# A fused attention and two-layer MLP kernel: the first stage in a new order, the layer-norm weights moved into the weight split, and new first loads

## The chip, the cores and the metric

The kernel runs on one core of a Trainium2 chip. The metric is the device time of one execution in microseconds (us); the kernel before takes 528.44 us (median of 3 runs, 527.57 to 528.45).

The engines are named as the profile names them: PE (TensorE: matmuls; PEld is its weight load), DVE (VectorE), ACT (ScalarE), POOL (GpSimd) and SP (SyncE, which here only starts DMAs). ACT can start DMAs too.

## The reference

Three steps, each feeding the next; the reference computes them in 32-bit floats (weights arrive as 64-bit floats).

```python
# 1. attention: batch 2, 8 heads, 768 positions, head size 64, n_global=8, n_local=96
scores = scale * q @ k^T
keep = (column < n_global) | (0 <= row - column < n_local)
scores = scores - slope[head] * dist          # dist: n_local for global columns, else |row - column|
a = softmax(where(keep, scores, -1e9)); x = a @ v          # x: 1536 tokens x 512
# 2. first layer: d_ff = 1024
h = x @ w_in; u = h * softmax(h)
ln = (u - mean(u)) / sqrt(var(u) + 1e-6) * g_ln
x2 = ln @ w_out
# 3. second layer: d_ff = 2048
g = x2w * sigmoid(x2w) with x2w = x2 @ w2_in;  out = g @ w2_out
```

## The kernel before

The 1536 tokens are 12 tiles of 128; tiles 0 and 6 begin a batch and see one key tile, the others two (their own and the one before). Each 32-bit matmul of the two layers is done as three matmuls of halves: both operands are split in a high part `hi` and a remainder `lo`, and hi*hi + hi*lo + lo*hi is summed in PSUM.

**The weights** come as 64-bit words in units of 128x512 numbers (512 KB). Units 0 to 7 are `w_in` (0 to 3 for the first 512 columns, 4 to 7 for the rest), 8 to 15 `w_out`, 16 and up the second layer. Each unit is loaded (`u_load`, five buffers), its upper words scaled (`u_exp`, on POOL, ACT or DVE), put together by three bit passes on DVE (`u_bits`, L139, L141, L143), and split (`u_hi`, L124 or L126; `u_lo`, L162). The units of `w_out` are multiplied by `g_ln` between (`u_gain`, L154).

**The first stage**, for each tile: scores of heads 0 to 3 and of heads 4 to 7 (`scores`, L275); on DVE the bias and the row's maximum for each head (`smax`, L294); on ACT exp with the row's sum (`sexp`, L300); two small DVE instructions for the sums' reciprocals (`ssum`); the multiplication of each head by it (`snorm`, on POOL or DVE, L126: called a norm below); transposes (L322), their copies out of PSUM (`transA_out`, ACT), the product with v (`av`, L341), its split (ACT, then DVE); then the two halves of the hidden layer (`hmm`, L380, 12 matmuls each), the layer norm (`ln_max`, `ln_exp`, `ln_u`, `ln_s`, `ln_sq`, `ln_c` with a power of -0.5 on POOL, L420; `ln_d` on POOL, L424 and L425), its transpose (L435), and, for two tiles together, the two halves of `w_out` (`x2`, L455, 48 matmuls each).

**The order of the work** is written out: `ORDER` is a list of some 860 tokens such as `d3:5` (bias and maximum of head 3, tile 5), which Python calls one after another. Each engine executes its own instructions in that order; a wait on one engine holds all that stands behind it there. The same holds for the two DMA queues (SP and ACT). PSUM has four buffers `p`, so a group of matmuls also waits until an earlier group has been read. Ahead of the list stand the loads of the two counts (`ints`, L629 and L630) and the masks.

**The second stage** (from the matmuls of L518 on) runs in two groups of 768 tokens; the remaining units are prepared in its background.

Of the kernel before, what the change touches and what calls it, by code (L numbers as in the profile page):

```python
# [53 lines left out]


@with_exitstack
def kernel(ctx, tc, q, k, v, n_global, n_local, w_in, w_out, g_ln, w2_in, w2_out, out):
    nc = tc.nc
    B, H, S, D = 2, 8, 768, 64
    NT, DM = out.shape  # L60
    FF = w_in.shape[1]
    FF2 = w2_in.shape[1]
    NTILE = NT // 128
    TB = S // 128
    KD = DM // 128
    KF = FF // 128
# [791 lines left out]
```

## Time and profile before

| | |
|---|---|
| median of 3 runs | 528.44 us (527.57 to 528.45) |
| the profiled execution | 527.69 us; its span 525.6 us |
| PE busy | 495.4 us, 94% of the span |
| DVE, ACT, POOL busy | 311.9, 236.4 and 157.7 us |
| PE's share of the chain that ended last | 88% |

The page shows the span in 40 slices of 13.1 us: PE stands at 9 tenths or more from the fourth slice to the last but one, with one slice at 7 (near 225 us). A busy PE is not PE at its peak: the granted clock has a row of its own and is below full speed in the third slice.

### The profile page before, as it was taken

How to read it: one execution, taken by the hardware profiler on the slowest of the kernel's cores; microseconds unless marked ns; L12 is line 12 of the kernel's file. 1: busy time of each engine (PE TensorE's matmuls, PEld its weight loads, DVE VectorE, ACT ScalarE, POOL GpSimd, SP SyncE). 2: the span in 40 equal slices, each digit the busy share in tenths (PEclk: the TensorE clock that was granted, in tenths of full speed). 3: DMA queues.
4: the chain of work that ended last, by engine and by line, in shares of the span. 5: the costliest groups of instructions: out<-in, count | busy, mean ns of one | idle time of the engine just before them, and what ended most of it. 6: DMA issues, size and time to landing. Idle time of an engine off the chain costs nothing.

```text
span 525.6 us, 8114 instructions
## 1 busy us (share of the span) xinstructions
PE 495.4 (94%) x3025; PEld 436.1 (83%) x3025; DVE 311.9 (59%) x721; ACT 236.4 (45%) x532; POOL 157.7 (30%) x205
## 2 busy tenths in 40 slices
PE   1779999999999999979999999999999999999993
PEld 1457778889889889879999898989899898989982
DVE  4868888966566767974569898883441313122231
ACT  4866778554555645623245545443431212222121
POOL 2787968932222334151223242332000000000000
PEclk9969999999999999999999999999999999999998
DMA  7955524321304100202133433300030000000003
GB/s 197 296 168 144 172 67 122 101 63 59 121 1 141 42 19 24 81 4 77 42 98 110 153 108 133 121 1 2 0 121 2 0 1 0 1 0 1 1 1 126
DMA packets 27488, 38.37 MB, mean 73 GB/s; under 512 B 2864, under 2 KB 15152, under 8 KB 27440
## 3 DMA queue, kind: packets, MB, share of 16 engines
q1 hardware_dynamic: 27296, 37.24, 22.7%
q8 instruction: 26, 0.43, 0.3%
q10 hardware_dynamic: 144, 0.52, 0.3%
q14 instruction: 22, 0.18, 0.1%
HBM read 34.61 MB, written 3.15 MB: 72 GB/s over the span
## 4 chain that ended last, share of the span: by engine, by line
PE 88%; DVE 4%; POOL 3%; issue 2%; SPq 1%; DMA 1%; ACT 0%; DVEq 0%; POOLq 0%
PE p L518 26%; PE p L569 25%; PE p L455 12%; PE p L380 10%; PE p L275 4%; PE p L322 4%; PE p L341 4%; PE p L435 2%; DMA rq<-in_q_dram 1%; POOL st L420 1%; DVE A L294 1%; POOL A L126 1%; SPq L119 1%; POOL e L425 1%; DVE st L390 0%
## 5 line engine op out<-in xcount | busy, mean ns | idle before, releaser
L533 DVE SCALAR_TENSOR_TENSOR e<-e,p 128x384 f32<-128x384 f32 x64 | 32.6, 551 | 125.8 <-ACT e L527 125.8
L527 ACT ACTIVATE e<-p 128x384 f32<-128x384 f32 x64 | 28.0, 489 | 134.0 <-PE p L518 134.0
L569 PE MATMUL p<-w3h,gl 128*128 128x512 f32 x192 | 75.8, 395 | 0.0
L569 PE MATMUL p<-w3l,gh 128*128 128x512 f32 x192 | 75.7, 394 | 0.0
L569 PE MATMUL p<-w3h,gh 128*128 128x512 f32 x192 | 75.4, 393 | 0.0
L143 DVE SCALAR_TENSOR_TENSOR cc<-cx,cc 128x512 uint32<-128x512 uint32 x48 | 58.5, 1221 | 0.2
L518 PE MATMUL p<-x2h,w2h 128*128 128x384 f32 x256 | 55.6, 338 | 0.0
L518 PE MATMUL p<-x2l,w2h 128*128 128x384 f32 x256 | 55.5, 338 | 0.0
L518 PE MATMUL p<-x2h,w2l 128*128 128x384 f32 x256 | 55.4, 338 | 0.0
L300 ACT ACTIVATE A<-A,negmax 128x256 f32<-128x256 f32 (+1 forms) x96 | 46.2, 483 | 14.3 <-DVE negmax L294 13.9
L380 PE MATMUL p<-wih,xT 128*128 128x512 f32 x192 | 50.7, 406 | 0.0
L126 POOL TENSOR_SCALAR A<-A,sm 128x256 f32<-128x256 f32 (+1 forms) x71 | 40.5, 582 | 31.1 <-DVE sm L305 25.9
L518 PEld LDWEIGHTS p<-x2h,w2h 128*128 128x128 f32 x256 | 46.1, 188 | 2.6
L518 PEld LDWEIGHTS p<-x2l,w2h 128*128 128x128 f32 x256 | 46.0, 188 | 0.0
L518 PEld LDWEIGHTS p<-x2h,w2l 128*128 128x128 f32 x256 | 45.8, 188 | 0.0
L294 DVE CUSTOM_DVE_ANT_0 A<-p,bias 128x256 f32<-128x256 f32 (+1 forms) x96 | 34.8, 395 | 16.9 <-PE p L322 6.3
L569 PEld LDWEIGHTS p<-w3h,gl 128*128 128x128 f32 x192 | 36.1, 188 | 8.3
L569 PEld LDWEIGHTS p<-w3l,gh 128*128 128x128 f32 x192 | 36.0, 188 | 7.3
L569 PEld LDWEIGHTS p<-w3h,gh 128*128 128x128 f32 x192 | 36.1, 188 | 7.2
L380 PEld LDWEIGHTS p<-wih,xT 128*128 128x128 f32 x192 | 34.5, 189 | 9.0 <-issue 1.7
L275 PE MATMUL p<-rk,rq 64*128 64x256 f32 (+1 forms) x192 | 29.6, 441 | 11.2 <-DMA rk<-in_k_dram 9.0
L162 POOL TENSOR_TENSOR w3l<-cc,w3h 128x512 fp32r<-128x512 f32 x16 | 23.5, 1468 | 52.0 <-ACT w3h L124 48.6
(106 smaller groups left out, 839.6 us busy)
## 6 DMA issues: line engine op xcount, KB each, us to landing
cx<-in_moe_w_out_dram SPq DMA_DIRECT2D x24, 512.0 KB, 3.4
cx<-in_moe_w_in_dram SPq DMA_DIRECT2D x23, 512.0 KB, 3.8
rq<-in_q_dram SPq DMA_DIRECT2D x12, 256.0 KB, 4.6
rk<-in_k_dram SPq DMA_DIRECT2D x12, 256.0 KB, 4.9
vf<-in_v_dram SPq DMA_DIRECT2D x12, 256.0 KB, 5.4
out_dram<-x2T SPq DMA_DIRECT2D x12, 256.0 KB, 3.2
cx<-in_moe_w_in_dram ACTq DMA_DIRECT2D x1, 512.0 KB, 5.6
ints<-in_n_local_dram SPq DMA_DIRECT2D x1, 1.0 KB, 5.0
```

The costliest lines, as they stand in the source:

```text
L126: eng.tensor_scalar(out=out, in0=in_, scalar1=scale, scalar2=1.0, op0=ALU.mult, op1=ALU.mult)
L143: V.scalar_tensor_tensor(out=y, in0=x[:, :, 1].bitcast(U32), scalar=0x80000000, in1=y, op0=ALU.bitwise_and, op1=ALU.bitwise_or)
L162: eng.tensor_tensor(out=lo, in0=w, in1=f(hi), op=ALU.subtract)
L275: nc.tensor.matmul(p[:, a, j, 0:128 * len(ks)], lhsT=rq[z, t % 2, pr, :], rhs=rk[z, W, pr, :], start=True, stop=True)
L294: nc.vector.tensor_tensor_reduce(out=x[:, c, 0:n], in0=p[:, a, j, 0:n], in1=bb, scale=-0.125, scalar=1e30, op0=ALU.add, op1=ALU.min, accum ...
L300: nc.scalar.activation(out=x[:, c, 0:n], in_=x[:, c, 0:n], func=ACTF.Exp, bias=negmax[:, t * H + h:t * H + h + 1], scale=-1.0, accum_out=s ...
L380: nc.tensor.matmul(p[:, half, :], lhsT=x[:, a, kk, :], rhs=w[:, kk, n], start=(i == 0), stop=(i == 11))
L455: nc.tensor.matmul(p[:, d], lhsT=x[:, kk, c], rhs=y[:, kk, sl], start=(i == 0), stop=(i == 3 * KF - 1))
L518: nc.tensor.matmul(p, lhsT=w[m // 2][:, kk, c], rhs=x[:, kk, s * HG:(s + 1) * HG], start=(i == 0), stop=(i == 11))
L527: nc.scalar.activation(out=e, in_=p2[:, s, 0:HG], func=ACTF.Tanh, scale=0.5)
L533: nc.vector.scalar_tensor_tensor(out=e, in0=e, scalar=1.0, in1=p2[:, s, 0:HG], op0=ALU.add, op1=ALU.mult)
L569: nc.tensor.matmul(o, lhsT=x[:, c], rhs=w[m // 2][:, m % 2, :], start=(m == 0 and i == 0), stop=(last and i == 2))
```

## The change

- `ORDER` is a new list; each token's work may move on its engine.
- **Norms on three engines**: `m0a` to `m7a` put a norm on ACT. Before, 71 of the 96 were on POOL and 25 on DVE; now 36 are on POOL, 34 on ACT and 26 on DVE.
- **Layer-norm weights**: `u_gain` is gone. `u_hi` of a `w_out` unit now multiplies by `g_ln` (two ACT instructions of 256 numbers in place of one of 512), and `u_lo` does so too (two DVE `scalar_tensor_tensor`). Before, seven of these eight units were multiplied and seven subtracted on POOL; now no `w_out` unit uses POOL for either.
- **First loads**: k of tiles 0 and 1 and unit 2 are started by ACT, the rest by SP; the two counts come as one row each and are spread over the 128 partitions by a matmul (`counts_all`, and a copy out of PSUM); `g_ln` comes as 8 rows of 128 numbers and is transposed by a matmul, where it was a load of 1,024 single numbers.
- **Masks**: the second set of bias products is spread over ACT, DVE and POOL (`bba`, `bbv`, `bbp`).
- **Layer norm**: the power and the following product are a token of their own (`lp`), and `ln_d` runs on POOL (7 tiles), ACT (3) or DVE (2).

The diff, cut to its core (the list of tokens to its first lines):

```diff
-cl:0 lq:0 lk:0 cep:0 c1:0 ba:0 sb:0 bb:0 c2:0 cl:1 sa:0 c3:0 d0:0 d4:0 cep:1 d1:0 d5:0 d2:0 lk:1 d6:0 c1:1 d3:0 lq:1 kg:0 c2:1 bc:0 cl:2 d7:0 lq:2
...
+ints:0 lka:0 ni:0 nb:0 lq:0 mk:0 cla:2 ml:0 cl:3 sb:0 bbv:6 bbp:7 sa:0 bbp:1 bbv:2 ba:0 lq:1 bbp:0 d0:0 lka:1 cep:2 d4:0 cl:0 x0:0 cl:6 d1:0 d5:0 d2:0
...
-    ints = per.tile([128, 4], I32, name="ints")
+    ints = per.tile([1, 4], I32, name="ints")
+    intf = per.tile([1, 4], F32, name="intf")
+    one = per.tile([1, 128], F32, name="one")
+    g8 = per.tile([8, 128], F32, name="g8")
...
-    def u_gain(i, eng):
-        w, g = u_parts(i)[0], units[i][3]
-        for j in range(units[i][1]):
-            eng.tensor_scalar(out=w[:, j], in0=w[:, j], scalar1=g[:, j:j + 1], scalar2=1.0, op0=ALU.mult, op1=ALU.mult)
-
     def u_hi(i, eng=None):
         w, hi, _ = u_parts(i)
-        scaled(hi, w, eng)
+        g = units[i][3]
+        if g is None:
+            scaled(hi, w, eng)
+        else:
+            for j in range(units[i][1]):
+                scaled(hi[:, j], w[:, j], eng, g[:, j:j + 1])
 
     def u_lo(i, eng):
         w, hi, lo = u_parts(i)
-        eng.tensor_tensor(out=lo, in0=w, in1=f(hi), op=ALU.subtract)
+        g = units[i][3]
+        if g is None:
+            eng.tensor_tensor(out=lo, in0=w, in1=f(hi), op=ALU.subtract)
+        else:
+            for j in range(units[i][1]):
+                eng.scalar_tensor_tensor(out=lo[:, j], in0=w[:, j], scalar=g[:, j:j + 1], in1=f(hi[:, j]), op0=ALU.mult, op1=ALU.subtract)
         ustate.pop(i)
...
+    def counts():
+        nc.sync.dma_start(out=ints[:, 0:2], in_=n_local.bitcast(I32).rearrange("(a n) -> a n", a=1))
+        nc.sync.dma_start(out=ints[:, 2:4], in_=n_global.bitcast(I32).rearrange("(a n) -> a n", a=1))
...
+    def counts_all():
+        mt["p"] = psum()[:, 0, 0:4]
+        nc.tensor.matmul(mt["p"], lhsT=one, rhs=intf, start=True, stop=True)
...
+    def gains():
+        nc.sync.dma_start(out=g8, in_=g_ln.rearrange("(k p) -> k p", p=128))
+
+    def gains_t():
+        mt["g"] = psum()[:, 0, 0:KF]
+        nc.tensor.transpose(mt["g"], g8, ident[0:KF, 0:KF])
...
-        nc.gpsimd.tensor_tensor(out=col[6], in0=col[6], in1=mhalf, op=ALU.pow)
-
-    def ln_d(t):
+
+    def ln_r(t):
         u, col = ys[t]
-        nc.gpsimd.tensor_tensor(out=col[6], in0=col[6], in1=col[4], op=ALU.mult)
-        nc.gpsimd.tensor_scalar(out=u, in0=u, scalar1=col[2], scalar2=col[6], op0=ALU.add, op1=ALU.mult)
+        P = nc.gpsimd
+        P.tensor_tensor(out=col[6], in0=col[6], in1=mhalf, op=ALU.pow)
+        P.tensor_tensor(out=col[6], in0=col[6], in1=col[4], op=ALU.mult)
+        if f"lda:{t}" in toks:
+            P.tensor_tensor(out=col[7], in0=col[6], in1=col[2], op=ALU.mult)
+
+    def ln_d(t, eng=None):
+        u, col = ys[t]
+        if eng is None:
+            nc.scalar.activation(out=u, in_=u, func=ACTF.Identity, bias=col[7], scale=col[6])
+        else:
+            eng.tensor_scalar(out=u, in0=u, scalar1=col[2], scalar2=col[6], op0=ALU.add, op1=ALU.mult)
         ys[t] = u
...
-        nc.sync.dma_start(out=ints[:, 0:2], in_=n_local.bitcast(I32).partition_broadcast(128))
-        nc.sync.dma_start(out=ints[:, 2:4], in_=n_global.bitcast(I32).partition_broadcast(128))
...
-            if x == "lk:0":
-                nc.sync.dma_start(out=gt, in_=g_ln.rearrange("(k p) -> p k", p=128))
```

How the order moves, in three places (each row is an instruction's line, its operation, what it writes and reads, its size, and how many follow each other).

ACT from its first instruction, before: `cx` is a weight unit, `bias_92` and `bias` the bias products, `A` the scores, `wih` a split unit, `ath` transposed scores copied out.

```order
L119 DMA cx<-in_moe_w_in_dram 128x1024
L124 ACT_TABLE_LOAD
L124 ACTIVATE bias_92<-dm 128x128 x8
L124 ACTIVATE bias<-dm 128x256 x8
L300 ACTIVATE A,sm<-A,negmax 128x128 x8
L124 ACTIVATE wih<-cc 128x512 x2
L124 ACTIVATE ath<-p 128x512
```

And now:

```order
L208 DMA rk<-in_k_dram 128x4x128
L123 DMA cx<-in_moe_w_in_dram 128x1024
L128 ACT_TABLE_LOAD
L128 ACTIVATE bias_95<-dm 128x128 x8
L208 DMA rk<-in_k_dram 128x4x128
L333 ACTIVATE A,sm<-A,negmax 128x128 x3
L128 ACTIVATE bias<-dm 128x256
L333 ACTIVATE A,sm<-A,negmax 128x128 x5
L128 ACTIVATE A<-A,sm 128x128 x3
L128 ACTIVATE wih<-cc 128x512
L128 ACTIVATE A<-A,sm 128x128 x2
```

The exps of tile 0 (L300, now L333) stand behind 8 and 1 bias products where they stood behind 16; k of tile 1 is started between them, and five norms of tile 0 (`A<-A,sm`) follow on ACT.

POOL, the norms of tiles 0 and 1, before: `wil` is the remainder of a `w_in` unit, `kg`, `rk` and `vg` copies of the global keys and values.

```order
L126 TENSOR_SCALAR A<-A,sm 128x128 x4
L126 TENSOR_SCALAR cc<-cx 128x512
L162 TENSOR_TENSOR wil<-cc,wih 128x512 x2
L126 TENSOR_SCALAR A<-A,sm 128x256 x7
L126 TENSOR_SCALAR vg<-vf 8x512
L126 TENSOR_SCALAR A<-A,sm 128x256
```

And now:

```order
L130 TENSOR_SCALAR A<-A,sm 128x128 x3
L168 TENSOR_TENSOR wil<-cc,wih 128x512
L130 TENSOR_SCALAR cc<-cx 128x512
L130 TENSOR_SCALAR rk<-kg 128x4x8
L168 TENSOR_TENSOR wil<-cc,wih 128x512
L130 TENSOR_SCALAR cc<-cx 128x512
L130 TENSOR_SCALAR A<-A,sm 128x256 x4
```

Tile 1 had all its eight norms (128x256) on POOL; now it has four there, three on ACT and one on DVE.

POOL near the end of the first stage, the layer norms of tiles 10 and 11, before: `st` holds the tile's small columns (L420 is the power), `e` the tile, `w3l` and `w2l` remainders of second-layer units.

```order
L420 TENSOR_TENSOR st<-st,mhalf 128x1
L162 TENSOR_TENSOR w3l_2271<-cc,w3h_2270 128x512
L424 TENSOR_TENSOR st<-st 128x1
L425 TENSOR_SCALAR e<-e,st 128x1024
L162 TENSOR_TENSOR w2l_2269<-cc,w2h_2268 128x512
L420 TENSOR_TENSOR st<-st,mhalf 128x1
L424 TENSOR_TENSOR st<-st 128x1
L425 TENSOR_SCALAR e<-e,st 128x1024
```

And now:

```order
L457 TENSOR_TENSOR st<-st,mhalf 128x1
L458 TENSOR_TENSOR st<-st 128x1
L460 TENSOR_TENSOR st<-st 128x1
L168 TENSOR_TENSOR w2l_2264<-cc,w2h_2263 128x512
L457 TENSOR_TENSOR st<-st,mhalf 128x1
L458 TENSOR_TENSOR st<-st 128x1
L467 TENSOR_SCALAR e<-e,st 128x1024
```

A remainder no longer stands between the power and the product; the large multiplication of tile 10 is gone from POOL (it is on ACT), that of tile 11 stays. On DVE the four subtractions of the second layer's input (L501, now L543), which stood together between the columns of tiles 10 and 11, stand two and two around tile 11's column.

## Rows read from the trace of the kernel before

**Rows 1.** By stretch: window, length, busy PE, PEld, DVE, ACT, POOL (xinstructions), clock, DMA.

```profile
0.00:9.00 9.00, 0.00 (x0) 0.02 (x1) 2.29 (x10) 1.30 (x2) 1.91 (x10) 1.00 0.59 149
9.00:40.90 31.90, 23.07 (x136) 17.02 (x137) 25.96 (x87) 24.17 (x78) 23.35 (x33) 0.84 0.76 240
40.90:109.50 68.60, 67.82 (x504) 55.67 (x503) 57.02 (x165) 50.90 (x121) 53.32 (x78) 1.00 0.38 111
109.50:220.00 110.50, 110.50 (x838) 95.41 (x837) 74.99 (x226) 58.03 (x134) 31.22 (x51) 1.00 0.20 61
220.00:236.00 16.00, 12.53 (x105) 12.32 (x104) 12.12 (x22) 6.78 (x11) 8.74 (x5) 1.00 0.09 33
236.00:517.00 281.00, 281.00 (x1449) 255.67 (x1449) 138.42 (x218) 94.64 (x188) 39.16 (x29) 1.00 0.14 47
```

**Rows 2.** What PE waited for in the whole span: total us, times, longest.

```profile
PE p L275 <- DMA rk<-in_k_dram: 9.0, 1, 9.0
PE p L322 <- POOL A L126: 4.6, 4, 3.4
PE p L435 <- POOL e L425: 3.6, 2, 3.5
PE p L341 <- DVE negmax L294: 2.5, 1, 2.5
PE p L275 <- DMA rq<-in_q_dram: 2.2, 1, 2.2
```

**Rows 3.** Timeline of POOL after 23 us: start, duration (us), instructions [idle before].

```profile
23.56 5.26 POOL L126 TENSOR_SCALAR A<-A,sm 128x256 f32<-128x256 f32 x7 [1.12 <-DVE sm L305]
```

**Rows 4.** Timeline near 225 us, POOL, DVE and PE.

```profile
221.71 4.48 POOL L420 TENSOR_TENSOR st<-st,mhalf 128x1 f32<-128x1 f32 x1 [10.87 <-DVE st L419]
...
222.22 3.55 DVE L501 TENSOR_TENSOR x2l<-x2T,x2h 128x768 fp32r<-128x768 f32 x4
...
229.38 1.10 PE L435 MATMUL p<-ident,e 128*128 128x128 f32 x8 [3.47 <-POOL e L425]
...
236.98 0.55 POOL L420 TENSOR_TENSOR st<-st,mhalf 128x1 f32<-128x1 f32 x1 [6.42 <-DVE st L419]
```

**Rows 5.** Timeline of SP, the queue of the first loads.

```profile
1.19 0.41 SPq L630 DMA_DIRECT2D ints<-in_n_global_dram  x1
...
3.22 3.75 SPq L119 DMA_DIRECT2D cx<-in_moe_w_in_dram  x1
```

**Rows 6.** DMA issues of the page: kind, count, KB each, median us to landing.

```profile
out_dram<-x2T SPq DMA_DIRECT2D x12, 256.0 KB, 3.2
```

**Rows 7.** Timeline of DVE in the first 12 us.

```profile
7.02 0.17 DVE L226 CAST nlf<-ints 128x4 f32<-128x4 int32 x1 [4.75 <-DMA ints<-in_n_global_dram]
...
9.26 0.42 DVE L139 TENSOR_SCALAR cc<-cc 128x512 uint32<-128x512 uint32 x1
...
10.44 0.69 DVE L143 SCALAR_TENSOR_TENSOR cc<-cx,cc 128x512 uint32<-128x512 uint32 x1
11.24 0.29 DVE L294 CUSTOM_DVE_ANT_0 A<-p,bias 128x128 f32<-128x128 f32 x1
```

**Rows 8.** Instructions to 109.5 us by line and form: count, busy us, mean ns, idle before.

```profile
L126 POOL TENSOR_SCALAR A<-A,sm 128x256 f32<-128x256 f32 x39 | 24.9, 651 | 6.9 <-DVE sm L305 4.0 <-ACT A L300 3.0
L143 DVE SCALAR_TENSOR_TENSOR cc<-cx,cc 128x512 uint32<-128x512 uint32 x16 | 13.4, 845 | 0.1
L141 DVE SCALAR_TENSOR_TENSOR cc<-cx,cc 128x512 uint32<-128x512 uint32 x16 | 12.9, 814 | 0.2
L162 POOL TENSOR_TENSOR wol<-cc,woh 128x512 fp32r<-128x512 f32 x7 | 10.5, 1507 | 0.0
L139 DVE TENSOR_SCALAR cc<-cc 128x512 uint32<-128x512 uint32 x16 | 9.2, 577 | 1.6 <-POOL cc L126 1.1 <-ACT cc L124 0.3
L154 POOL TENSOR_SCALAR cc<-cc,gt 128x256 f32<-128x256 f32 x14 | 7.9, 580 | 0.9 <-DVE cc L143 0.8
```

**Rows 9.** Timeline of ACT from 8 us.

```profile
8.98 4.16 ACT L124 ACTIVATE bias<-dm 128x128 bf16<-128x128 f32 x16 [6.53 <-DVE dm L234]
```

More of the change, by code (lines that the diff above doesn't have):

```diff
@@ L60 @@
     NT, DM = out.shape
+    toks = ORDER.split()
     FF = w_in.shape[1]
@@ L190, with load @@
     rq = at.tile([128, 2, H // 2, 128], F32, name="rq")
-    def load(nm, t):
+    def load(nm, t, eng=nc.sync):
         if nm == "v":
             vt[t] = at2.tile([128, DM], F32, tag="v", name="vf", bufs=4)
-            nc.sync.dma_start(out=vt[t], in_=v[t])
+            eng.dma_start(out=vt[t], in_=v[t])
         else:
@@ L243, in masks2 @@
-    def masks2(eng=None):
-        dm = dms[0]
-        for h in range(H):
-            scaled(bias[:, h, 0:2, :], dm[:, 0:2, :], eng, -(2.0 ** (2 - h)))
-    def masks3():
-        nc.vector.tensor_copy(bias[:, :, 2, :], bias[:, :, 0, :])
+        z = 2 if c else 0
+        if c:
+            V.tensor_copy(nlf, mt.pop("p"))
+        V.tensor_scalar(out=mk[:, c, :], in0=rf[:, c, :], scalar1=nl, scalar2=1e30, op0=ALU.is_ge, op1=ALU.mult)
+        V.scalar_tensor_tensor(out=mk[:, z, :], in0=rf[:, 2, :], scalar=ng, in1=mk[:, c, :], op0=ALU.is_ge, op1=ALU.mult)
@@ new lines, in mask_rows, with bias_first, bias_head @@
+        if c:
+            V.scalar_tensor_tensor(out=dm[:, 2, :], in0=rf[:, 1, :], scalar=nl, in1=mk[:, 2, :], op0=ALU.min, op1=ALU.max)
+        else:
+            V.scalar_tensor_tensor(out=dm[:, 0:2, :], in0=rf[:, 0:2, :], scalar=nl, in1=mk[:, 0:2, :], op0=ALU.min, op1=ALU.max)
+    def bias_first():
+        for h in range(H):
+            scaled(bias0[:, h, :], mt["dm"][:, 2, :], None, -(2.0 ** (2 - h)))
+    def bias_head(h, eng=None):
+        scaled(bias[:, h, 0:2, :], mt["dm"][:, 0:2, :], eng, -(2.0 ** (2 - h)))
@@ L600 @@
     OPS = dict(
-        lk=lambda t: load("k", t), lq=lambda t: load("q", t), lv=lambda t: load("v", t),
-        ba=lambda t: masks1(), bb=lambda t: masks2(), bc=lambda t: masks3(),
+        ints=lambda _: counts(), ni=lambda _: counts_f(), nb=lambda _: counts_all(), mk=lambda _: mask_rows(1), ml=lambda _: mask_rows(0),
+        ba=lambda _: bias_first(), g8=lambda _: gains(), gm=lambda _: gains_t(), gt=lambda _: gains_out(), cl=u_load, cla=lambda i: u_load(i, nc.scalar),
         kg=k_global, vg=v_global, sa=lambda t: scores(t, 0), sb=lambda t: scores(t, 1),
@@ L617 @@
     )
+    for n in "qkv":
+        OPS[f"l{n}"] = lambda t, n=n: load(n, t)
+        OPS[f"l{n}a"] = lambda t, n=n: load(n, t, nc.scalar)
+    for e, eng in (("a", None), ("v", V_), ("p", P_)):
+        OPS[f"bb{e}"] = lambda h, eng=eng: bias_head(h, eng)
+        OPS[f"bc{e}"] = lambda _, eng=eng: bias_wrap(eng)
+        OPS[f"ld{e}"] = lambda t, eng=eng: ln_d(t, eng)
     for i in range(8):
+        OPS[f"m{i}a"] = lambda t, i=i: snorm(t, i, None)
         OPS[f"d{i}"] = lambda t, i=i: smax(t, i)
@@ L628 @@
     with tc.manual_schedule():
-        nc.sync.dma_start(out=ints[:, 0:2], in_=n_local.bitcast(I32).partition_broadcast(128))
-        nc.sync.dma_start(out=ints[:, 2:4], in_=n_global.bitcast(I32).partition_broadcast(128))
         masks()
-        for x in ORDER.split():
+        for x in toks:
             nm, t = x.split(":")
```

122 lines of the change are left out of this document (61 added, 61 removed).

## The prediction

> **What bounds the kernel now.** I read the busy time by stretch first [rows 1]. From 236 us on PE is busy all the time (281.00 of 281.00), and the change moves nothing there but the background units; from 109.5 to 220 us it is busy 110.50 of 110.50. So all that can be won stands in three places: the 9.0 us before the first matmul, the 31.9 us after it with PE busy 23.07 and a granted clock that averages 0.84, and the 16 us from 220 us with PE busy 12.53. After 40.9 us PE hardly waits, so what the first stage wins by then it keeps only if no later matmul has to wait; a later wait is lost for good.
>
> Then the list of PE's waits [rows 2]: 9.0 us for the first keys, 2.2 us for the second queries, 4.6 us for norms on POOL, 2.5 us at the product with v, and 3.6 us for the layer norm on POOL. Two rows show the causes. In the timeline of POOL seven norms of tile 1 follow one another for 5.26 us while PE waits [rows 3]. Near 225 us a power of 128x1 numbers takes 4.48 us where the next one takes 0.55; beside it DVE runs four subtractions for 3.55 us, and PE then waits 3.47 us for the tile [rows 4].
>
> **The start.** The counts' second DMA begins at 1.19 us and SP's sixth DMA is stuck for 3.75 us [rows 5]. The trace has no load of a single row. From above: it lands no sooner than now. From below: the quickest median landing on the page is 3.2 us [rows 6], which gives 4.4 us. I take 4.4, since that row is a DMA without company and the new one has a single row. DVE works on the counts from 7.02 us and on the first scores from 11.24 us, after three passes on a unit that begin at 9.26 us [rows 7], which the new order puts behind. So DVE starts 2.6 us sooner. The matmul and the copy that spread the counts cost well under 1 us and lie in this; that of `g_ln` waits for the eighth DMA on SP and stands ahead of tile 1's scores. k of tile 1 is started by ACT behind eight bias products and, on ACT's queue, behind unit 3's landing; tile 1's scores come hardly sooner than now. The gain of the start is therefore DVE's and ACT's time, not PE's directly.
>
> **Norms and weights: whose work decides.** I compare both orders at tile 5's first hidden half, which PE begins at 109.5 us. DVE has been busy for 85.3 us by then (2.29 + 25.96 + 57.02), ACT for 76.4, POOL for 78.6 [rows 1].
>
> POOL loses 27 of its norms by that place, at 651 ns, both gain instructions of seven units (7.9 us) and seven subtractions (10.5 us) [rows 8]: 17.6 + 7.9 + 10.5 = 36.0 us; five bias products come back, at about 0.5 us (below a norm's 0.65) 2.5 us. It keeps 45 us and bounds nothing.
>
> ACT gains 20 norms. The nearest rows: a bias product takes 0.26 us (16 in 4.16) [rows 9], POOL's norm 0.65. At 0.4 us that is 8 us, so 85 of some 103 us: not the bound.
>
> DVE gains the eight `w_out` remainders with the weights in them. Nearest rows: a two-input pass of the same size undisturbed, 0.69 us [rows 7], and POOL's subtraction, 1.51 us [rows 8]. I take 0.75 each (it is the DVE's own form in two pieces): 6.0 us. Ten further ones are drawn ahead of that place (four norms, one split and its subtraction, a row maximum of 1,024, a score maximum, two bias products); at about 0.5 us, between the passes of 0.42 and 0.69, they are 5.0 us. Against it DVE is less disturbed: its 48 passes take 845, 814 and 577 ns on the mean [rows 8] against 0.69, 0.69 and 0.42 undisturbed [rows 7], 16 x (0.155 + 0.124 + 0.157) = 7.0 us in all. POOL's work falls by 33.5 of 78.6, so I take back 43% of it, 3.0 us. DVE needs 85.3 + 11.0 - 3.0 = 93.3 us by that place.
>
> PE has 12 matmuls fewer ahead of it (tile 6's half transposes and a half of tile 7's scores moved behind), at 0.135 us (67.82 / 504) 1.6 us. If the first stage gains g, tile 5's hidden half begins at 109.5 - 1.6 - g = 107.9 - g, and that must leave DVE its 93.3 us and its idle time. So **g = 14.6 - idle**. DVE's idle time now is 6.7 us in the first stretch, 5.9 in the second and 11.6 in the third. I take 4.1 for the first (2.6 less), 4 for the second (PE is still slow and waits for loads) and 2 for the third (where DVE is itself what PE waits for): 10, so g = 4.6 us. Ends: idle of 6, g = 8.6; idle of 14.6, g = 0.
>
> The new waits are then PE's on DVE and ACT between 20 and 100 us, short and many, where it now has few and long ones.
>
> **The end of the stage.** The excess of the power is 4.48 - 0.55 = 3.9 us, of which PE saw 3.47 [rows 4]. In the new order tile 10's power stands beside two unit passes and not four subtractions, its large multiplication is on ACT, and 100 matmuls, many of them short, lie between tile 10's hidden layer and its transpose, where now 73 do. Two passes are 1.4 us [rows 7]. I take a gain of 2.7 us, with 0 and 3.5 as ends.
>
> That rests on the one row. The Trainium skill (SBUF — State Buffer, section Who interferes with whom) says that a DVE instruction with two SBUF inputs contends with a POOL instruction that reads SBUF, and the later of the two blocks fully. The trace agrees in this one place: 4.48 us beside four such subtractions. By that rule the change also puts more such instructions on DVE (the eight remainders), and two subtractions again stand ahead of tile 11's power; what it would make of the time is rival 2's.
>
> **The sum.** Against the profiled execution: 527.69 - 4.6 - 2.7 = 520.4 us. Its span is 525.6, with 2.1 us around it that stay. It lies 0.75 us below the median of the runs, 528.44, so I forecast 520.4 + 0.7 = **521.1 us**. With both ends: 4.6 and 2.7 become 8.6 and 3.5, 516.3 us, or 0 and 0, 528.4 us.
>
> **Rivals.**
> 1. *The second queue brings nothing.* The first 9 us move 149 GB/s, later stretches 240 [rows 1], which speaks for a start that was held up by small pieces and against this rival; the keys' 9.0 us [rows 2] are ended by a landing, which speaks for it. If the counts and keys come 0.8 us sooner and not 2.6, idle is 11.8, g = 2.8, and the time 522.9 us. The Trainium skill (DMA: Bandwidth & Descriptors, section Issuing engines are not separate DMA queues) says that DMAs of all issuers run on the same 16 engines, so that several issuers save only the time to issue. No run here shows it yet.
> 2. *The wait of the power comes back*, at tile 10 or 11, since DVE's work still stands beside it: gain at the end 0, 523.8 us. For it: the one row of 4.48 us. Against it: the subtractions stand apart.
> 3. *Slower: DVE loses as much time as now.* Place: tiles 2 to 5. If its idle time after 9 us does not shrink (17.5 us) because each wait for scores, ACT and POOL stays, idle is 21.6, g = -7.0, and the time 528.44 + 7.0 - 2.7 = 532.7 us. It decides from an idle time of 14.6 + 2.7 = 17.3 us on. For it: ACT and DVE are both fuller than before at every tile. Against it: of the third stretch's idle time most is DVE waiting for PE, which goes when DVE is late.
> 4. *Nothing to see:* the order is only dealt out differently, idle comes near 17.3, and the time is 528.4 us.
>
> **Chances.** What a measurement of this kernel can tell from no change is about 0.2%, 1.06 us. Forecast (516.3 to 527.3) 0.56; rival 1 0.14; rival 2 0.12; rival 3 0.12; rival 4 0.06. Faster by over 0.2%: 0.56 + 0.14 + 0.12 = 0.82; the same 0.06; slower 0.12. The range leaves out rival 3 and a little below the lower end: 515.8 to 528.6 us.
>
> **What would show it.** Right: the first score maximum on DVE before 9 us; tile 0's hidden half (40.9 us now) between 33 and 38 us; norms on POOL no longer the name of PE's longest wait; POOL's busy time to tile 5's hidden half near 45 us and DVE's near 93; a power near 0.6 us and PE's wait for the last layer norms under 1 us; the second stage as long as now. Wrong: PE waits of over 5 us together between 45 and 110 us (DVE's or ACT's names on them), the second stage longer, or a first matmul no sooner than now.

## The result and the profile after

| | before | after |
|---|---|---|
| median | 528.45 us (4 runs, 527.57 to 528.63) | 516.06 us (4 runs, 515.14 to 516.54) |
| ratio, 95% interval | | 0.9767, 0.9748 to 0.9785 |
| profiled execution, its span | 527.69, 525.6 us | 515.70, 513.9 us |
| busy PE, DVE, ACT, POOL | 495.4, 311.9, 236.4, 157.7 us | 485.1, 312.6, 254.3, 111.9 us |

The change takes 12.4 us off; 7.3 were forecast. The new lines of the same places: scores L308 (L275 before), the bias and row maximum L327, norms L128 and L130, transposes L355, product with v L374, hidden layer L413, power L457, layer-norm transpose L477, second stage L560 (up-projection, the product with `w2_in`) and L611 (down-projection, with `w2_out`).

Where it went is read from four marks in PE's timeline: the first hidden half of tile 0, that of tile 5, the first matmul of the down-projection, and the last one.

| from, to | before | after | gained |
|---|---|---|---|
| start, tile 0's first hidden half | 40.92 | 35.52 | 5.40 |
| on to tile 5's | 68.43 | 67.83 | 0.60 |
| on to the first down-projection | 147.46 | 145.04 | 2.42 |
| on to the last matmul | 260.65 | 257.49 | 3.16 |
| the end of the span, and what lies outside | 10.23 | 9.82 | 0.41 |

Busy time by stretch, first of before (stretches that [rows 1] doesn't have), then of after; the columns are as in [rows 1].

```profile
109.35:256.81 147.46, 143.99 (x1095) 128.66 (x1094) 96.25 (x264) 69.55 (x153) 42.53 (x60) 1.00 0.18 56
256.81:517.46 260.65, 260.65 (x1298) 234.91 (x1296) 129.85 (x199) 90.06 (x179) 36.59 (x25) 1.00 0.14 47
```

```profile
0.00:9.00 9.00, 1.33 (x8) 1.27 (x10) 4.10 (x15) 2.99 (x9) 3.58 (x14) 1.00 0.75 223
9.00:35.50 26.50, 17.28 (x135) 13.11 (x131) 21.34 (x78) 20.95 (x65) 17.12 (x21) 0.94 0.72 229
35.50:103.35 67.85, 65.39 (x488) 54.31 (x489) 63.03 (x187) 58.43 (x145) 26.14 (x43) 1.00 0.46 146
103.35:248.39 145.04, 143.66 (x1107) 130.22 (x1106) 91.69 (x252) 82.45 (x186) 29.21 (x47) 1.00 0.14 45
248.39:505.88 257.49, 257.49 (x1298) 233.45 (x1296) 131.71 (x203) 88.91 (x176) 35.80 (x25) 1.00 0.15 49
```

Two readings. PE idles 2.5 us between tile 0's and tile 5's hidden halves (65.39 of 67.85 us busy) and idled 0.8 before, so what was won by tile 5 was won ahead of tile 0's mark; the 0.60 us come with fewer matmuls in that stretch (488 recorded, 504 before). And the second stage runs the same 1,298 matmuls with PE busy throughout, at a granted clock of 1.00 in both, and is 3.16 us shorter, though the change does nothing there but deal out the background units.

PE's waits after, against [rows 2]:

```profile
PE p L308 <- DMA rq<-in_q_dram: 4.5, 1, 4.5
PE p L248 <- DVE intf L244: 3.2, 1, 3.2
PE p L308 <- DMA rk<-in_k_dram: 3.0, 1, 3.0
PE p L279 <- DMA g<-in_moe_g_ln_dram: 2.7, 1, 2.7
PE p L355 <- POOL A L130: 2.6, 1, 2.6
PE p L477 <- ACT e L465: 1.2, 1, 1.2
PE p L355 <- ACT ath L128: 1.1, 1, 1.1
```

And PE's timeline of the head (start, duration, instructions, idle before):

```profile
8.26 2.08 PE L308 MATMUL p<-rk,rq 64*128 64x128 f32 x16 [4.47 <-DMA rq<-in_q_dram]
13.07 0.24 PE L279 MATMUL p<-ident,g 8*128 8x8 f32 x1 [2.73 <-DMA g<-in_moe_g_ln_dram]
16.34 2.08 PE L308 MATMUL p<-rk,rq 64*128 64x256 f32 x8 [3.02 <-DMA rk<-in_k_dram]
...
26.51 3.54 PE L355 MATMUL p<-ident,A 128*128 128x128 f32 x16 [2.55 <-POOL A L130]
...
35.52 2.14 PE L413 MATMUL p<-wih,xT 128*128 128x512 f32 x8 [0.46 <-DVE negmax L327]
```

The first scores wait for q of tile 0, which SP issues at 1.42 us and which lands near 8.1 us; tile 1's scores come at 16.34 us, three us later than before, because ACT issues k of tile 1 only at 9.46 us, when unit 3 has landed (POOL starts on it at 9.52). One wait for POOL's norms is left, and most of the transposes behind it run at 1.2 GHz: the granted clock is 0.5 from 26.70 to 30.12 us.

### The profile page after: what moved, and what is told of

Read it like the earlier page. It is cut to its first block, busy times and chain, and to the rows that moved or that the text cites. A ratio compares the mean times of both kernels' runs of the same rounds, so it can differ in the third digit from the quotient of the medians.

```text
span 513.9 us, 8122 instructions
## 1 busy us (share of the span) xinstructions
PE 485.1 (94%) x3028; PEld 432.4 (84%) x3028; DVE 312.6 (61%) x735; ACT 254.3 (49%) x580; POOL 111.9 (22%) x150
## 4 chain that ended last, share of the span: by engine, by line
PE 85%; DVE 8%; DMA 2%; ACT 1%; issue 1%; POOL 0%; SPq 0%; DVEq 0%
PE p L560 26%; PE p L611 26%; PE p L497 12%; PE p L413 9%; PE p L308 4%; PE p L355 3%; PE p L374 3%; PE p L477 2%; DVE A L327 2%; DMA rq<-in_q_dram 1%; DMA rk<-in_k_dram 1%; DVE cc L147 1%; DVE cc L145 1%; DVE cc L143 1%; ACT A L333 1%
## 5 line engine op out<-in xcount | busy, mean ns | idle before, releaser
L611 PE MATMUL p<-w3h,gl 128*128 128x512 f32 x192 | 75.3, 392 | 0.0
L611 PE MATMUL p<-w3l,gh 128*128 128x512 f32 x192 | 75.2, 392 | 0.0
L611 PE MATMUL p<-w3h,gh 128*128 128x512 f32 x192 | 74.7, 389 | 0.0
L147 DVE SCALAR_TENSOR_TENSOR cc<-cx,cc 128x512 uint32<-128x512 uint32 x48 | 60.9, 1270 | 0.3
L560 PE MATMUL p<-x2h,w2h 128*128 128x384 f32 x256 | 55.2, 337 | 0.0
L560 PE MATMUL p<-x2l,w2h 128*128 128x384 f32 x256 | 55.0, 335 | 0.0
L560 PE MATMUL p<-x2h,w2l 128*128 128x384 f32 x256 | 54.7, 334 | 0.0
L333 ACT ACTIVATE A<-A,negmax 128x256 f32<-128x256 f32 (+1 forms) x96 | 46.0, 481 | 13.3 <-DVE negmax L327 11.7
L413 PE MATMUL p<-wih,xT 128*128 128x512 f32 x192 | 50.6, 405 | 0.5 <-DVE negmax L327 0.5
L327 DVE CUSTOM_DVE_ANT_0 A<-p,bias 128x256 f32<-128x256 f32 (+1 forms) x96 | 34.3, 395 | 23.1 <-PE p L355 14.6
L560 PEld LDWEIGHTS p<-x2h,w2h 128*128 128x128 f32 x256 | 45.6, 188 | 2.3
L560 PEld LDWEIGHTS p<-x2l,w2h 128*128 128x128 f32 x256 | 45.9, 188 | 0.0
L560 PEld LDWEIGHTS p<-x2h,w2l 128*128 128x128 f32 x256 | 45.3, 188 | 0.0
L611 PEld LDWEIGHTS p<-w3h,gl 128*128 128x128 f32 x192 | 36.0, 188 | 7.6
L611 PEld LDWEIGHTS p<-w3l,gh 128*128 128x128 f32 x192 | 36.0, 188 | 6.9
L611 PEld LDWEIGHTS p<-w3h,gh 128*128 128x128 f32 x192 | 36.1, 188 | 6.8
L413 PEld LDWEIGHTS p<-wih,xT 128*128 128x128 f32 x192 | 34.3, 189 | 8.5 <-DVE negmax L327 0.9
L110 ACT ACTIVATE gh<-e 128x384 fp32r<-128x384 f32 x60 | 29.7, 526 | 18.6 <-DVE e L575 18.6
L145 DVE SCALAR_TENSOR_TENSOR cc<-cx,cc 128x512 uint32<-128x512 uint32 x48 | 34.1, 716 | 0.0
L111 DVE TENSOR_TENSOR gl<-e,gh 128x384 fp32r<-128x384 f32 x60 | 30.8, 555 | 3.8
```

Source lines behind the costliest of these rows:

```text
L110: nc.scalar.activation(out=hi, in_=src, func=ACTF.Copy)
L111: nc.vector.tensor_tensor(out=lo, in0=src, in1=f(hi), op=ALU.subtract)
L145: V.scalar_tensor_tensor(out=y, in0=x[:, :, 0].bitcast(U32), scalar=29, in1=y, op0=ALU.logical_shift_right, op1=ALU.bitwise_or)
L147: V.scalar_tensor_tensor(out=y, in0=x[:, :, 1].bitcast(U32), scalar=0x80000000, in1=y, op0=ALU.bitwise_and, op1=ALU.bitwise_or)
L327: nc.vector.tensor_tensor_reduce(out=x[:, c, 0:n], in0=p[:, a, j, 0:n], in1=bb, scale=-0.125, scalar=1e30, op0=ALU.add, op1=ALU.min, accum ...
L333: nc.scalar.activation(out=x[:, c, 0:n], in_=x[:, c, 0:n], func=ACTF.Exp, bias=negmax[:, t * H + h:t * H + h + 1], scale=-1.0, accum_out=s ...
```

## The experiments

Each run was compared with the kernel before on the same chip; its ratio to that kernel is what can be compared between runs on different chips. The marks are from each run's own trace.

| run | median us | ratio (95%) | first scores | tile 1's | tile 0's hidden half | from there to the last matmul |
|---|---|---|---|---|---|---|
| the change | 516.06 | 0.9767 (0.9748 to 0.9785) | 8.26 | 16.34 | 35.52 | 470.36 |
| e5 the change again | 515.96 | 0.9756 (0.9731 to 0.9782) | 7.12 | 16.78 | 36.01 | 470.39 |
| e3 early norms on POOL | 519.33 | 0.9837 (0.9806 to 0.9867) | 7.95 | 16.67 | 38.04 | 470.56 |
| e4 late norms on POOL | 517.77 | 0.9799 (0.9770 to 0.9829) | 7.27 | 17.32 | 37.13 | 470.67 |
| e6 k of tile 1 first | 512.20 | 0.9674 (0.9648 to 0.9700) | 7.15 | 9.90 | 32.53 | 470.43 |
| e7 one queue | 514.36 | 0.9723 (0.9695 to 0.9752) | 5.33 | 15.42 | 34.60 | 470.36 |
| e9 keys, queries, then units | 511.87 | 0.9674 (0.9661 to 0.9688) | 5.61 | 7.81 | 33.00 | 469.83 |
| e10 gain on POOL again | 529.80 | 1.0007 (0.9993 to 1.0020) | 7.36 | 16.32 | 35.91 | 482.87 |
| e8 power beside subtractions | 515.27 | 0.9737 (0.9707 to 0.9768) | 8.47 | 16.68 | 36.25 | 470.35 |
| e11 the same behind a shift | 516.78 | 0.9759 (0.9744 to 0.9774) | 8.01 | 16.52 | 36.79 | 470.34 |
| e1 after with 32 bytes more | 517.79 | 0.9804 (0.9778 to 0.9830) | 7.52 | 16.48 | 36.76 | 471.78 |
| e2 before with 32 bytes more | 525.65 | 0.9954 (0.9940 to 0.9968) | 9.11 | 13.17 | 40.65 | 475.56 |
| e12 before, x2 moved 32 bytes | 527.58 | 0.9962 (0.9950 to 0.9974) | 9.06 | 13.75 | 41.30 | 477.50 |
| before | 528.45 | 1 | 9.01 | 13.31 | 40.92 | 476.54 |

**The yardstick, e5.** No edit.

> The changed kernel once more, as the yardstick for the kernels beside it: in the earlier ones the same instructions ahead of tile 0's hidden half took 35.5, 36.8 and 37.1 us, so its first 35 us are expected to differ by a us or so from one execution to the next. Both theories: 515 to 517 us, and a second stage of 257.5 us.

515.96 us. The head differs by a us between executions of the same instructions (35.5 to 36.8 us in e1, e5, e8, e11 and the first profile, 37.1 in e4, whose order differs only later); the rest doesn't (470.3 to 470.4 us in all of these but e1 and e4).

### Why the second stage is shorter: e1, e2, e12

The change adds three tiles to the pool `per`: `intf` (32 bytes of each partition with its slot), `one` and `g8` (512 each). In the compiled program the weights of pairs 2 to 7 of the second stage, which lie on the left above `per`, thus begin at byte 27,872 and not 26,816; by 128 the remainder is 96 and not 64. Pairs 0 and 1, x2h, gh and gl lie on the right and stay, at a remainder of 96.

```diff
     flag = per.tile([1, 1], I32, name="flag")
+    pad = per.tile([128, 8], F32, name="pad")
```

> The changed kernel with one unused tile of 32 bytes per partition behind the last tile of pool per, so that every tile on the left above it, the weight pairs 2 to 7 of the second stage among them, lies 32 bytes higher; no instruction changes. Theory (where tiles lie): the second stage was 3.2 us shorter after the change because its new tiles in per moved those weights by 1,056 bytes; another 32 bytes give the old remainder by 64 back, so the span from the first matmul of line 611's counterpart to the last is 260.7 us again and not 257.5, a step of 42 matmuls takes 8.43 us and not 8.30 from the third step on, and the time is 519.2 us. Rival (the background units or the engines beside PE in that stage are dealt out better): nothing moves, 516.1 us, 8.30 us a step.

> The kernel before with the same unused tile of 32 bytes and nothing else. Theory (where tiles lie): the second stage shrinks by 3.2 us, 8.30 us a step all through, 525.2 us. If the place matters only by the larger shift (1,056 bytes and not the 32 in it): 528.4 us. Rival (background units): 528.4 us.

e2's second stage takes 257.48 us and not 260.65: all of the 3.2 us, with nothing changed but a place by 32 bytes. So both of its expectations of no gain are out. e1's takes 258.96 and not 257.49: the place costs again, but 1.5 us, half of what was expected. Single steps show which matmuls it is. First before, a down- and an up-projection of pairs 2 and up; then after, then e1:

```profile
323.87:328.06 4.19, 4.19 (x19) 1.00 0.44 147
328.06:332.31 4.25, 4.25 (x26) 1.00 0.31 90
```

```profile
314.83:318.95 4.12, 4.12 (x19) 1.00 0.51 174
318.95:323.14 4.19, 4.19 (x25) 1.00 0.29 83
```

```profile
316.22:320.41 4.19, 4.19 (x20) 1.00 0.47 158
320.41:324.59 4.18, 4.18 (x26) 1.00 0.31 84
```

Of a matmul's two operands one is loaded into PE first and held (`lhsT` in the kernel), the other is streamed past it (`rhs`). Before, both projections are 0.06 to 0.07 us longer; in e1 (remainder 0) only the down-projection is, which streams these weights; the up-projection, which holds them, is not. e12 moves what the up-projection streams, from a remainder of 96 to 64, in the kernel before:

```diff
                 x2l = wk.tile([128, KD, G], F32R, name="x2l")
+                pad = wk.tile([128, 8], F32, name="pad")
```

> The kernel before with an unused tile of 32 bytes behind x2h and x2l, which moves these two (what the up-projection streams) 32 bytes down and nothing else that a matmul reads. Theory A (weights and streamed tile must have the same remainder of their address by 128): the up-projection of weight pairs 2 to 7 is fast (2.5 to 2.7 us of the 3.2 stay with the down-projection's share taken out: about 1.7 us less), that of pairs 0 and 1 slow, and the time is 527 us. Theory B (only the place of the weights counts): nothing moves, 528.5 us and steps of 8.43 us as before.

An up- and a down-projection of pair 1, then a down- and an up-projection of pairs on the left, then the whole stage:

```profile
264.00:268.16 4.16, 4.16 (x25) 1.00 0.51 162
276.41:280.50 4.09, 4.09 (x19) 1.00 0.54 176
318.06:322.26 4.20, 4.20 (x20) 1.00 0.48 168
322.26:326.44 4.18, 4.18 (x26) 1.00 0.30 100
259.91:518.80 258.89, 258.89 (x1298) 1.00 0.14 47
```

The up-projection on the left falls from 4.25 to 4.18 us, so the place of the streamed tile counts as well and theory B is out. Theory A has the size (1.8 us less), but it wanted pairs 0 and 1 slow, and pair 1 takes 4.16. That tiles' places set 3.2 us here is shown; the rule by which they do is not.

The time of e2 fell by 2.4 us, not 3.2. Its profile has a loss of 1.5 us near 230 us that the profile of the kernel before has not (under the hardware below); e12's has it too, so the kernel before may lose it in other executions, and what e2's median lacks is not explained.

### What set the head: e3, e4, e6, e7, e9

```diff
-m0a:0 ... m7a:2
+m0p:0 ... m7p:2
```

> The changed kernel with the 12 ACT norms of tiles 0 to 2 back on POOL, in the same places of the order. Theory (the lead is won before tile 0's hidden half, by the norms of the first tiles; after it PE is busy anyway): POOL gets some 12 x 0.61 = 7.3 us more in the first 45 us, PE waits for POOL's norms again, tile 0's hidden half moves from 35.5 us to 38 or 40, and most of that stays: 518 to 521 us. Rival (what counts is each engine's sum up to tile 5, of which POOL has plenty): 516 us, within 0.7.

> The changed kernel with the 22 ACT norms of tiles 3 to 11 back on POOL, those of tiles 0 to 2 left on ACT. Theory (the lead is won before 35.5 us and PE is busy after it): 516 to 517 us, PE's waits between 35 and 220 us longer by under 1 us together. Rival (sums up to tile 5): POOL gets 13 us more, DVE and ACT less, and the time moves by 2 us or more, either way.

e3 went as the theory had it: tile 0's hidden half at 38.04 us, 519.33 us. PE's longest wait has its old name again, in e3's waits and timeline:

```profile
PE p L355 <- POOL A L130: 7.3, 5, 4.9
```

```profile
29.21 3.68 PE L355 MATMUL p<-ident,A 128*128 128x128 f32 x16 [4.85 <-POOL A L130]
```

e4 moved nearly twice as many norms, and behind tile 0's hidden half it costs 0.3 us (470.67). Its time lies above the 516 to 517 us expected; against e5 the trace puts 1.1 us of that ahead of tile 0's hidden half, where its order is the change's own, so that part is not the norms' doing, and PE's waits from 35 to 220 us are no longer than in the change's profile. The norms of the first three tiles matter, and those of the later nine hardly do, as far as this one trace shows. Even with the early norms back on POOL tile 0's hidden half begins 2.9 us sooner than before the change (38.04 against 40.92 us); what of this the counts, the masks and the order of ACT's first work earned, no run separates.

```diff
-ints:0 lka:0 ni:0 nb:0 lq:0 mk:0 cla:2 ml:0 cl:3 ... lq:1 bbp:0 d0:0 lka:1 ... g8:0
+ints:0 lka:0 ni:0 nb:0 lq:0 lka:1 mk:0 lq:1 cla:2 g8:0 ml:0 cl:3 ... bbp:0 d0:0
```

> The changed kernel with the loads of q and k of tile 1 and of g_ln ahead of the two weight units that now stand ahead of them (k of tile 1 right behind k of tile 0 on ACT's queue). Theory (the head is set by tile 1's scores, which wait for k of tile 1 until 16.3 us, and by the slow matmuls after the wait that follows): tile 1's scores start near 11 us, the wait of 2.6 us for POOL's norms near 25 us and the stretch at a granted clock of 0.5 behind it shrink, tile 0's hidden half moves from 35.5 to 32 or 33 us, and the time is 512.5 to 514 us. Rival (the DMA engines are full from 9 to 20 us, so the units come later by as much, and DVE waits for them): 516 us, within 0.7.

512.20 us: 3.8 below e5 on the same chip, with no instruction removed. The wait for POOL's norms falls from 2.6 to 0.7 us, but PE now waits 1.9 us for ACT's. The granted clock, 0.5 from 26.70 to 30.12 us in the profile after, stays at 1.00 in e6 from its first record, at 22.86 us, on. After, then e6, PE alone, 24 to 32 us (window, busy, clock, DMA share, GB/s):

```profile
24.00:28.00 4.00, 1.49 (x8) 0.84 0.44 134
28.00:32.00 4.00, 4.00 (x34) 0.74 0.49 135
```

```profile
24.00:28.00 4.00, 2.96 (x22) 1.00 0.46 143
28.00:32.00 4.00, 3.90 (x48) 1.00 0.45 130
```

(The clock of a row is a mean.) Yet what e6 wins is idle time alone. From the start to tile 0's hidden half, e5, then e6:

```profile
0.00:36.01 36.01, 18.68 (x140) 0.95 0.69 224
0.00:32.53 32.53, 20.55 (x139) 1.00 0.77 249
```

PE idles 17.33 us in e5 and 11.98 in e6, but is busy 1.9 us longer: ahead of e6's first clock record eight scores of 64x256 still take 2.08 us (at 20.71 us), and in the profile after eight such scores take 1.14 (at 22.82). So the late k of tile 1 cost a wait; that the clock's later fall cost time on top, these runs do not show.

```diff
-ints:0 lka:0 ... cla:2 ... lka:1
+ints:0 lk:0 ... cl:2 ... lk:1
```

> The changed kernel with its three early loads of ACT's queue issued by SP, in the same order. Theory (two queues only save the time to issue, some 0.5 us each, and the order of the loads decides): 515.5 to 517 us. Rival (the second queue is what brought the first scores from 9.0 to 8.3 us and freed the later loads): the first matmul of the scores at 9 us or later and 517.5 us or more.

With all loads on SP the first scores come at 5.33 us and the time is 514.36 us, 1.6 below e5. Neither expectation holds: the second queue saves no time here. The edit moves two things, though. In the change ACT's queue issues a weight unit at 1.20 us, ahead of q of tile 0 (1.42 us); here q goes ahead of every unit. e9 below has two queues with the units behind, and its first scores come at 5.61 us, so what delays q is the unit beside it, and not that there are two queues.

```profile
5.33 2.08 PE L308 MATMUL p<-rk,rq 64*128 64x128 f32 x16 [1.76 <-DMA rq<-in_q_dram]
15.25 0.24 PE L279 MATMUL p<-ident,g 8*128 8x8 f32 x1 [7.85 <-DMA g<-in_moe_g_ln_dram]
```

The Trainium skill (DMA: Bandwidth & Descriptors, section Issuing engines are not separate DMA queues) says that issuing from several engines saves only the time to issue, since all of them run on the same DMA engines. This run agrees: one queue in place of two costs nothing.

```diff
-ints:0 lka:0 ni:0 nb:0 lq:0 mk:0 cla:2 ml:0 cl:3 ... lq:1 bbp:0 d0:0 lka:1 ... bbp:4 c2:2 ... g8:0 ... gt:0
+ints:0 lka:0 ni:0 nb:0 lq:0 lka:1 mk:0 lq:1 g8:0 cl:2 ml:0 cl:3 ... bbp:0 d0:0 ... bbp:4 c2:2 gt:0
```

> The changed kernel with k of tiles 0 and 1 alone on ACT's queue, q of tiles 0 and 1 and g_ln first on SP's, all weight units behind them on SP's, and the copy of g_ln moved ahead on DVE (the product of tile 0 with v waited 0.8 us for it in the run with k of tile 1 first). Theory (the head is set by when the loads land in the order in which PE asks for them): the first scores start near 5 us and tile 1's by 8 us, DVE's first score maximum stands near 7.5 us as in the run with one queue, tile 0's hidden half starts near 31 us, and the time is 510 to 511.5 us. Rival (DVE now waits for the units, which land later): tile 0's hidden half at 32.5 us or later and 512 us or more.

The loads land as hoped (first scores 5.61, tile 1's 7.81 us), the time does not follow: tile 0's hidden half at 33.00 us as the rival had it, 511.87 us, no better than e6. POOL's first unit waits 1.62 us for its load and DVE 1.09 us for POOL. PE, early, waits 3.72 us for tile 0's norms on ACT and 2.83 us for tile 1's on POOL, and then runs at 1.2 GHz (a granted clock of 0.50 from 24 to 28 us):

```profile
13.61 1.27 PE L355 MATMUL p<-ident,A 128*128 128x128 f32 x4 [3.72 <-ACT A L128]
23.44 3.68 PE L355 MATMUL p<-ident,A 128*128 128x128 f32 x16 [2.83 <-POOL A L130]
```

Here PE waits for norms, and the engines that make them for the units, no longer for the loads of k and q. e6 and e9, with the same ratio, beat both kernels: the changed one by 3.8 us (e6 against e5, on the same chip).

### The layer-norm weights: e10

```diff
-                scaled(hi[:, j], w[:, j], eng, g[:, j:j + 1])
+        scaled(hi, w, eng)
...
-c3:10
+c3:10 ugp:10
```

> The changed kernel with the layer-norm weights multiplied into the units by two POOL instructions of their own again, and the split and the subtraction as one instruction each over 512 numbers, on the engines that do them now. Theory (from tile 0's hidden half on PE is nearly always busy, so what the units cost DVE, ACT and POOL there does not show): 516 us within 0.8, DVE busy some 3 us less and POOL some 7 us more. Rival (each engine's sum up to tile 5 counts): 513 to 514 us, since DVE has 3 us less to do, or 518 us, if POOL's norms come late again.

529.80 us: both theories missed by far, and the whole gain is lost. The timeline of POOL, then of PE, shows the largest part of it:

```profile
49.95 1.04 POOL L158 TENSOR_SCALAR cc<-cc,gt 128x256 f32<-128x256 f32 x2 [5.29 <-DVE cc L147]
50.97 0.61 POOL L130 TENSOR_SCALAR vf<-vg 8x512 f32<-8x512 f32 x1
```

```profile
51.63 3.60 PE L369 MATMUL p<-ath,vf 128*64 128x128 f32 x32 [5.88 <-POOL vf L130]
```

POOL stands idle 5.29 us in front of the first multiplication, waiting for DVE's last pass on that unit; the copy that PE's product with v needs stands behind it on POOL. Further on PE waits 1.97 and 2.85 us for norms on POOL, and its granted clock averages 0.57 from 48 to 56 us. This is the place that I gave these tokens, not a cost that the kernel before paid there, so the run does not price the merging of the weights. It shows that a token on POOL is paid by what it waits for and by who stands behind it: 16 instructions of some 0.5 us, on an engine that is busy 56.2 of its first 116.3 us, cost 12.5 us from tile 0's hidden half on.

### The power near 225 us: e8, e11

```diff
-xs0:0 sq:11 fl:0 c2:23 xs1:0 lc:11 ulp:21 lp:11 Y00v:4 Y10v:3 X1:4 xs2:0 Y11a:3 Y01a:4 xs3:0 ldp:11
+xs0:0 sq:11 xs2:0 fl:0 c2:23 lc:11 xs1:0 xs3:0 ulp:21 lp:11 Y00v:4 Y10v:3 X1:4 Y11a:3 Y01a:4 ldp:11
```

(e11 also moves `c1:23`, a shift on DVE, in between `lc:11` and `xs1:0`, and `c2:23`, the next pass on that unit, behind the stretch shown.)

> The changed kernel with the four subtractions of the x2 split put right behind DVE's last small step of tile 11's layer norm, so that POOL's power of tile 11 stands beside all four of them as tile 10's did before the change. Theory (a power of 128x1 numbers is held up by DVE's subtractions): the power takes 3.5 to 4.5 us and not 0.56; since 1.2 us stand between the norm and its transpose now and the power starts 1 us sooner, PE waits 0 to 2 us for it and the time is 516 to 518 us. Rival (the 4.48 us of before came from something else): the power takes under 1 us and the time is 516 us.

> As the kernel with the power beside the four subtractions, but with a one-input shift over 128x512 numbers between DVE's last small step of the layer norm and the four subtractions, as two such passes stood there before the change, so that the power arrives while that shift runs. Theory (a POOL instruction that arrives during a one-input pass of DVE gets no turn until the subtractions behind it are all done): the power takes 3.5 to 4.5 us. Rival (it gets its turn between two subtractions, as in the run before, where it took 1.20 us): under 2 us. The time in both cases 515 to 517 us.

e8, POOL and DVE, and then e11's:

```profile
222.60 1.20 POOL L457 TENSOR_TENSOR st<-st,mhalf 128x1 f32<-128x1 f32 x1 [9.61 <-DVE st L452]
...
224.42 2.56 POOL L467 TENSOR_SCALAR e<-e,st 128x1024 f32<-128x1024 f32 x1
...
222.44 3.55 DVE L543 TENSOR_TENSOR x2l<-x2T,x2h 128x768 fp32r<-128x768 f32 x4
```

```profile
223.13 0.67 POOL L457 TENSOR_TENSOR st<-st,mhalf 128x1 f32<-128x1 f32 x1 [9.63 <-DVE st L452]
...
224.41 3.35 POOL L467 TENSOR_SCALAR e<-e,st 128x1024 f32<-128x1024 f32 x1
...
223.30 3.56 DVE L543 TENSOR_TENSOR x2l<-x2T,x2h 128x768 fp32r<-128x768 f32 x4
```

The power is not held for 4 us in either, so both theories' sizes fail; e11's rival (under 2 us) held, and e8's 1.20 us lie over its rival's 1 us. It is the large multiplication behind it that ends about a us after DVE's last subtraction (225.99 and 226.86 us) instead of after its 1.2 us. Beside four subtractions POOL's layer norm ends late, but a different one of its instructions is caught; what decides which, these runs do not show. In three profiles of the kernel before (its own, e2's and e12's) it was the power, at 4.48 us each time. PE waits for tile 11's norm in neither run: it is ready in time.

## Why the prediction was right in its direction and too small

516.06 us lies 0.2 us below the forecast's range (516.3 to 527.3 us) and inside the wider one (515.8 to 528.6).

**The head, point by point.** The counts land by 2.99 us, sooner than the 4.4 taken. The first score maximum on DVE, forecast before 9 us, came at 10.49: q of tile 0 was late, a load that no term of the sum had. Tile 0's hidden half at 35.52 us lies in the forecast stretch, 33 to 38.

**"Whose work decides"** is the step that failed, though its number held by luck. Tile 5's hidden half was forecast at 107.9 - 4.6 = 103.3 us and began at 103.35 (4.4 us won, from before's own mark of 109.35). But DVE was busy 88.5 us by then and not 93.3, and idle 14.9 us and not 10: two errors of nearly 5 us that cancel. Two lines of DVE to 103.35 us (columns as in [rows 8]) show the largest terms:

```profile
L171 DVE SCALAR_TENSOR_TENSOR wol<-cc,gt,woh 128x256 fp32r<-128x256 f32 x16 | 8.1, 556 | 0.2 <-ACT woh L128 0.2
L143 DVE TENSOR_SCALAR cc<-cc 128x512 uint32<-128x512 uint32 x16 | 6.9, 434 | 0.0
```

The remainders cost 8.1 us (6.0 taken). The three passes give back 16 x (-0.018 + 0.063 + 0.143) = 3.0 us, as taken (845, 814 and 577 ns in [rows 8]; now 863, 751 and 434). The ten further instructions at 5.0 us were misjudged: by that mark DVE has run six norms, a split, a subtraction and two bias products more, but four score maxima fewer, and the unit of `w_out` that it multiplied and subtracted before is gone, so that these nearly cancel. The runs put another mechanism in its place: from tile 0's hidden half on, PE needs 469.8 to 470.7 us whatever norms and loads DVE, ACT and POOL are given (e3 to e9), so that in these runs only what is ahead of that mark moves the time; e10 shows that a long wait behind it counts too. Ahead of it the norms of the first tiles count (e3), and the order of the first loads (e6). POOL's busy time, forecast at 45 us, was 46.8; it bound nothing by its sum, and e10 shows that a low sum is no protection.

**The new waits** are short as forecast, but few: five on DVE and ACT between 20 and 100 us, 3.2 us together, of which one of 0.4 us lies between 45 and 110 us.

**The end of the stage**: 2.7 us was forecast. Behind tile 5's hidden half the lead grows by 2.42 us although 12 matmuls, 1.6 us, were moved behind that mark: 4.0 us. Of these 2.1 are PE's idle time (147.46 - 143.99 = 3.47 before, 145.04 - 143.66 = 1.38 after), so this term was mis-sized by 0.6 us. Which of the edits there earned the 2.1 us (the subtractions moved, no remainder behind the power, the multiplication on ACT) no run separates. The other 1.9 had no term: 12 more matmuls take 0.3 us less. Scores make up about half of it: they now come 16 in a row, in 2.00 us, where before seven of eight groups were of 8, in 1.13 us each. The rest is spread over transposes and layers, and its cause is open. The subtractions stood beside tile 10's norm; now they stand beside tile 11's, which has slack (e8 and e11 put all four beside it, and PE waits no longer), and for tile 10's PE waits 1.2 us, not under 1. The Trainium skill (SBUF — State Buffer, section Who interferes with whom) says that of two instructions that contend the later one blocks fully; the multiplications of e8 and e11 fit that. The power of [rows 4], which the prediction took to agree, begins half a us before the subtractions do, so that it was not the later one; and no run here shows why the power of e8 slipped in between two of them.

**"The second stage as long as now"** is the other step that failed: 3.16 us, priced at nothing, from 1,056 bytes of new tiles (e1, e2).

The sum of the misses: -0.2 at the head's mark, 1.3 behind it, 3.2 in the second stage, 0.4 at the end and outside: 4.7 us, and 12.0 - 7.3 = 4.7 us between the two profiled executions.

**The rivals.** Rival 1's condition came: DVE's first score maximum is 0.75 us sooner (10.49 against 11.24), not 2.6, and the second queue brought nothing (e7). Its 522.9 us did not come, since DVE's sum does not decide. Rival 2 did not come: the powers of tiles 10 and 11 take 0.93 and 0.56 us. Rival 3 needed 17.3 us of DVE's idle time; it was 14.9.

## What to carry to other kernels

Find the mark from which the bounding engine is busy to the end, and judge an edit by when that mark is reached and by waits behind it, not by other engines' sums. Ahead of it, issue loads in the order in which that engine asks for them, before large loads that nobody needs yet, and look at the second operand that it waits for as well as the first. When an edit adds tiles, compare the untouched stages too: places alone moved 3.2 us here, a quarter of the whole gain.

## What the runs showed of the hardware that was not expected

- **Where a tile lies changes a matmul's pace** by 1.5% (4.12 or 4.19 us for 18 matmuls) at a granted clock of 1.00, with nothing waiting. It hangs on both operands' places; the rule stays open.
- **A wait can cost more than itself.** Behind the wait of 3.45 us at the end of the first stage, e2's matmuls run slow, and its clock reads 0.81 and 0.76 from 228 to 236 us; in the kernel before's own profile, behind 3.47 us, it stayed at 1.00, and in e12's, behind 3.46, it reads 0.64 from 232 to 236 us. PE was busy 145.50 us from tile 5's hidden half to the down-projection in e2 and 143.99 before: 1.5 us.

```profile
229.81 1.38 PE L436 MATMUL p<-ident,e 128*128 128x128 f32 x8 [3.45 <-POOL e L426]
230.84 2.06 PE L456 MATMUL p<-lnh,woh 128*128 128x256 f32 x8
...
235.14 1.12 PE L456 MATMUL p<-lnh,woh 128*128 128x256 f32 x8
```

- **The first matmuls run at half pace, and the clock's row does not show it.** In the profile after, eight scores of tile 1 take 2.08 us at 16.34 us and eight of the same form 1.14 us at 22.82. The trace's first record of the clock begins between them, at 19.88 us; ahead of it the row prints 1.00 without a record. In e9 eight such scores take 2.08 us at 27.05 us too, where the granted clock is recorded as 0.5. So the first rows' 1.00, in [rows 1] too, is no reading.
- **A weight unit issued among the first loads delays them**: the first scores, which wait for q of tile 0, begin at 5.33 us where one queue issues k and q ahead of all units (e7) and at 5.61 where two queues do (e9), but at 7.1 to 8.5 us where ACT's queue issues a unit among them (the change and its repeats, e6).
